# Scores of late attention pairs: two row-tiled matmuls per block replaced by one full-array matmul on a block-diagonal q^T

## The chip, the core and the metric

The kernel runs on one core of a Trainium2 chip. The metric is the device time of one launch in microseconds. The kernel before takes 220.62 us, the median of three runs (220.38 to 220.83). The profiled execution took 220.13 us, of which the profile's span covers 218.4 us.

The engines by their short names in the profile: PE is TensorE's matmuls, PEld its weight loads, DVE is VectorE, ACT is ScalarE, POOL is GpSimd, SP is SyncE, which here only issues transfers.

## The reference

Sinkhorn-sorted block attention, followed by a two-layer FFN with a squared ReLU. The batch B is 4, heads H 8, sequence S 768, head size D 64; the sequence falls into 8 blocks of 96.

```python
P = sort_net                                   # [4, 8, 8, 8]
for _ in range(5):                             # softmax-like steps on rows and columns
    P = exp(P - max(P)); P = P / sum(P, -1); P = P / sum(P, -2)
k_sorted = einsum('bhij,bhjcd->bhicd', P, k_blocks)
v_sorted = einsum('bhij,bhjcd->bhicd', P, v_blocks)
scores = matmul(q_blocks, k_sorted^T) / sqrt(D)          # inside each block of 96
attn = softmax(scores)
x = matmul(attn, v_sorted)                     # -> [3072, 512], heads side by side
h = maximum(x @ w_in, 0)                       # w_in  [512, 2048]
out = (h * h) @ w_out                          # w_out [2048, 512]
```

## The kernel before

Two heads are handled together as a "pair", so there are 16 units (b, hp). The kernel writes its operations into a plan, and a planner in Python orders them for each engine before anything is built. PE has two streams: the attention pieces and the FFN pieces ("chunks", 224 in all, each of four matmuls of 384 or 512 columns; the very last ones of eight of 256). Each attention piece has a *due* time, counted in FFN chunks:

```python
# Plan.run, the choice on PE (cut)
if sa is not None and (sf is None or sa < sf - 0.02
                       or (att[0].due <= chunks and sa <= sf + 0.1)):
    pick = (sa, att)          # attention piece at the head of its queue
elif sf is not None:
    pick = (sf, ffn)          # otherwise the next FFN piece
```

The due times are a table: for each batch and stage one number per pair or group. The stages are K, V, N (sorting of k and v), Z (transposes of k and q by DMA), S (scores), T (transpose of v), A (attention times v), X (transpose of the result), L (loads of the next batch).

Ten of the 16 units, pairs 2 and 3 of batch 1 and all of batches 2 and 3, are "late": their sorted k and their q are transposed by DMA, issued from SP:

```python
def s_turn(b, hp):                                       # cut
    nc.sync.dma_start_transpose(                         # kx: k^T of both heads, 128 rows
        out=kx_r[kx][:, 0:128 * NA].rearrange("p (a x) -> p a x", a=NA),
        in_=kn_r[m].rearrange("p a e d -> p (a e d)"))
    nc.vector.tensor_copy(out=qi_r[n]..., in_=qkv[b][0][:, 2*hp:2*hp+2, :]...)
    tiles["qT", b, hp] = att.tile([128, NA, 128], BF16, tag="qT", name="qT", bufs=6)
    nc.sync.dma_start_transpose(                         # q^T of both heads, 128 rows
        out=tiles["qT", b, hp], in_=qi_r[n].rearrange("p a e d -> p (a e d)"))
```

Rows 0 to 63 of kx and of q^T belong to the first head of the pair, rows 64 to 127 to the second. The scores of half a unit (4 blocks, 2 heads) are eight matmuls; each uses 64 rows of the array, so that the two heads can run side by side:

```python
# s_sc, for each half hf of the unit (cut); NQ = 4, C0 = 16, NB = 8, BLK = 96
for n in range(NQ):
    for h in range(2):
        nc.tensor.matmul(
            out=scp[:, h, BLK * n:BLK * (n + 1)],
            lhsT=kx_r[u.kx][64 * h:64 * (h + 1), NQ * hf + n::NB],     # late: every 8th column
            rhs=qT[64 * h:64 * (h + 1), :, C0 * (NQ * hf + n): C0 * (NQ * hf + n + 1)],
            start=True, stop=True)
```

In the early units the weights are `u.ksT[..., ... : ... + 128]`, contiguous, and `rhs` is contiguous too. ACT takes the exponential from PSUM into `et`, one activation of 384 columns per head. Then `s_av` multiplies by v, eight matmuls per half with `et` as the weights, 65 columns each, the 65th being the sum for the softmax:

```python
nc.tensor.matmul(out=oup[:, h, 66 * n:66 * n + D + 1],
                 lhsT=et_r[u.et[hf]][:, h, BLK * n:BLK * n + 128],
                 rhs=vb_r[w][:, NQ * hf + n, 2 * (u.hp % 2) + h, 0:D + 1], start=True, stop=True)
```

The result is transposed into xT, and the FFN reads xT: "up" is L958 (w_in as weights, 384 columns of xT), "down" is L988 (the squared activation as weights, 512 columns of w_out; L1016 at the end, 256 columns). The score matmuls are L651, attention times v is L838, the sorting of late k and v on 32x32 tiles of the array is L739. L413 is a filler matmul on ones that keeps PE at work while the first, latency-bound part runs.

Of the kernel before, what the change touches and what calls it, by code (L numbers as in the profile page):

```python
# [8 lines left out]
FP32 = mybir.dt.float32  # L9
# [9 lines left out]


DUES = {
    (0, "K"): (-79.0, -7.0, -34.5, 2.5),
    (0, "S"): (-13.5, 0.5, 6.0, 9.0),
    (0, "T"): (-30.5, -2.0, 4.5, 10.5),
    (0, "A"): (2.5, 14.5, 10.5, 12.5),
    (0, "X"): (4.5, 17.5, 19.0, 19.5),
    (0, "W"): (5.5,),
    (1, "V"): (18.5, 21.0),
    (1, "Q"): (21.0,),
    (1, "N"): (None, 27.0),  # L30
    (1, "Z"): (None, None, 42.0, 42.5),
    (1, "S"): (26.0, 38.5, 43.0, 49.5),
    (1, "A"): (42.0, 38.5, 44.0, 50.0),
    (1, "X"): (52.5, 47.5, 46.5, 51.5),
    (2, "L"): (66.0,),
    (2, "N"): (70.5, 75.5),
    (2, "V"): (67.0, 84.0),
    (2, "Z"): (76.0, 83.5, 78.0, 97.0),
    (2, "S"): (87.5, 93.5, 99.5, 100.0),
    (2, "A"): (91.0, 94.5, 100.0, 102.5),  # L40
    (2, "X"): (100.0, 109.5, 108.0, 104.0),
    (3, "L"): (109.5,),
    (3, "N"): (123.0, 127.0),
    (3, "V"): (123.0, 131.5),
    (3, "Z"): (127.0, 130.0, 127.5, 144.5),
    (3, "S"): (132.5, 145.5, 148.5, 158.0),
    (3, "A"): (138.0, 156.0, 161.5, 160.0),
    (3, "X"): (158.0, 156.0, 194.0, 265.0),
}


# [132 lines left out]
def kernel(  # L184
# [10 lines left out]
    nc = tc.nc  # L195
# [32 lines left out]

    plan = Plan()
    rvn, rvb = Ring(2), Ring(3)  # L230
    r1, r2, rf, rh1, rh2, rob = Ring(1), Ring(2), Ring(3), Ring(3), Ring(2), Ring(3)
    rqT, rao, rks, rvs, ret = Ring(6), Ring(3), Ring(3), Ring(3), Ring(4)
    rkx, rkn, rqi = Ring(3), Ring(4), Ring(4)
    AD = ("ACT", "DVE")

    def cost_f(n):
# [54 lines left out]

    kn_r = [const.tile([128, NA, 2, D], BF16, name=f"kn{n}") for n in range(4)]
    qi_r = [const.tile([128, NA, 2, D], BF16, name=f"qi{n}") for n in range(4)]
    kx_r = []
    for n in range(3):
        kx = const.tile([128, 128 * NB], BF16, name=f"kx{n}")
# [8 lines left out]
    w_in_bf = const.tile([128, KC, d_ff], BF16)  # L305
    w_out_bf = const.tile([128, NT, d_model], BF16)
    xT = const.tile([128, KC, n_tok], BF16)
    w_all = const.tile([128, NH // 2, NB, C0], BF16)
    w_t = const.tile([128, NH // 4, 4, NB], BF16)
    qkv = {}  # L310
    holds = {}
# [45 lines left out]
    def make_mask(e):  # L357

        src, w = ident, 64
        while w >= 4:  # L360
            dst = {C0: mask, 4: mask_t}.get(w) or const.tile([128, w], BF16, name=f"fold{w}")
            nc.gpsimd.tensor_tensor(out=dst, in0=src[:, 0:w], in1=src[:, w:2 * w], op=ALU.add)
            src, w = dst, w // 2
        nc.gpsimd.tensor_copy(out=mask_1.rearrange("p (z y) -> p z y", y=4),
                              in_=mask.rearrange("p (y z) -> p z y", z=4))

# [14 lines left out]
    rs = const.tile([NH, NB], FP32)  # L381
    cs = const.tile([NH, NB], FP32)
    pf = const.tile([NH, NB, NB], BF16)
    sel = const.tile([32, 32, C0], BF16)
    pt = const.tile([128, NB, NH], BF16)
    p_ij = const.tile([NH, 2, NH], BF16)

# [129 lines left out]
    def s_q(b, hp, p0, p1, due=0, after=None, eng=AD):  # L517

        n = p1 - p0
        t = {}  # L520

        def mm(e):
            qb = qkv[b][0]
            if b == 0:
                t["p"] = psf.tile([128, NA, n], BF16, tag="pf", name="qtp")
            else:
                t["p"] = ps1.tile([128, NA, n], BF16, tag="p1", name="qtp")
            for a in range(NA):
                for h in range(2):
                    nc.tensor.transpose(  # L530
                        out=t["p"][64 * h:64 * (h + 1), a, :],
                        in_=qb[p0:p1, 2 * hp + h, D * a:D * (a + 1)],
                        identity=ident[p0:p1, p0:p1])
            if p0 == 0:
                tiles["qT", b, hp] = att.tile(
                    [128, NA, 128], BF16, tag="qT", name="qT", bufs=6)

        def ev(e):
            qT, src = tiles["qT", b, hp].rearrange("p a x -> p (a x)"), t["p"]
            if b == 0:  # L540
                copy(e, qT.rearrange("p (i c a) -> p i c a", a=NA, c=C0)
                     [:, p0 // C0:p1 // C0, :, :], src.rearrange("p a (i c) -> p i c a", c=C0))
            else:
                copy(e, qT.rearrange("p (i a c) -> p i a c", a=NA, c=C0)
                     [:, p0 // C0:p1 // C0, :, :], src.rearrange("p a (i c) -> p i a c", c=C0))

        if b == 0:
            dep = landed[b, 0, 0, p0]
        else:
            dep = landed[b, 0, HP * (2 * hp // HP), 0]  # L550
        ring = rf if b == 0 else r1
        s1, old = ring.take()
        if p0 == 0:
            qTs[b, hp], oldq = rqT.take()
        else:
            oldq = []
        pe = plan.add("PE", 0.04 + 0.0023 * n, mm, [dep, id_op] + old, due, mode="col")
        readers[b].append(pe)
        op = one_of(eng, cost_b(NA * n), ev, [pe, after] + oldq)
        ring.use(s1, pe, op)  # L560
        rqT.use(qTs[b, hp], op)
        return op
# [72 lines left out]
    def s_sc(u, due=0):  # L635
# [3 lines left out]
        for hf in u.halves:  # L639
# [2 lines left out]
            slot, old = r2.take()  # L642

            def mm(e, hf=hf, st=st, slot=slot):
                qT = tiles["qT", u.b, u.hp]
                if not u.tiled:
                    qT = qT.rearrange("p a x -> p (a x)").rearrange("p (i q) -> p i q", q=BLK)
                st["p"] = scp = p2[slot]
                for n in range(NQ):
                    for h in range(2):  # L650
                        nc.tensor.matmul(  # L651
                            out=scp[:, h, BLK * n:BLK * (n + 1)],
                            lhsT=(u.ksT[64 * h:64 * (h + 1), HS * hf + BLK * n:HS * hf + BLK * n + 128]
                                  if not u.tiled else
                                  kx_r[u.kx][64 * h:64 * (h + 1), NQ * hf + n::NB]),
                            rhs=(qT[64 * h:64 * (h + 1), NQ * hf + n, :] if not u.tiled else
                                 qT[64 * h:64 * (h + 1), :, C0 * (NQ * hf + n):
                                    C0 * (NQ * hf + n + 1)]),
                            start=True, stop=True)

            s2 = slot
            u.et[hf], olde = ret.take()
            pe = plan.add("PE", 0.17 if not u.tiled else 0.26, mm, [u.k_op, u.q_op] + old, due,
                          mode="row")
            r2.use(s2, pe)
            rqT.use(qTs[u.b, u.hp], pe)
            if not u.tiled:
                rks.use(u.n, pe)
            else:
                rkx.use(u.kx, pe)  # L670
            u.exps[hf] = []
            if u.b == 0:
                def ex(e, st=st, et=et_r[u.et[hf]]):
# [6 lines left out]
                continue  # L680
            for h in range(2):
                def ex(e, h=h, st=st, et=et_r[u.et[hf]]):
                    nc.scalar.activation(  # L683
                        out=et[:, h, 0:HS].rearrange("p (n c a) -> p n c a", c=C0, a=NA),
                        in_=st["p"][0:96, h, 0:HS].rearrange("p (n a c) -> p n c a", c=C0, a=NA),
                        func=AF.Exp, scale=scale)
                op = plan.add("ACT", cost_f(HS)[0], ex, [pe] + olde)
                r2.use(s2, op)
                u.exps[hf].append(op)
# [91 lines left out]
    def loaded(b):  # L781
        return landed[b, 0, HP, 0]

    def s_turn(b, hp):
# [21 lines left out]
        qp = plan.add("DVE", 0.5, q_pair, [landed[b, 0, HP * (2 * hp // HP), 0]] + oldi)  # L806
        readers[b].append(qp)
        rqi.use(n, qp)
        qTs[b, hp], oldq = rqT.take()

        def q_turn(e):
            tiles["qT", b, hp] = att.tile([128, NA, 128], BF16, tag="qT", name="qT", bufs=6)
            nc.sync.dma_start_transpose(
                out=tiles["qT", b, hp], in_=qi_r[n].rearrange("p a e d -> p (a e d)"))

        sp = plan.add("SP", 1.35, q_turn, [qp, loaded(b)] + oldq)
        q_op = plan.add("WAY", 1.4, lambda e: None, [sp])
        rqi.use(n, q_op)
        rqT.use(qTs[b, hp], q_op)
        return kx, k_op, q_op  # L820

    def s_av(u, due=0):
        nao, olda = rao.take()
# [3 lines left out]
        for hf in u.halves:  # L827
# [4 lines left out]
            def mm(e, hf=hf, st=st, slot=slot):  # L832
# [3 lines left out]
                for n in range(NQ):  # L836
                    for h in range(2):
                        nc.tensor.matmul(  # L838
                            out=oup[:, h, 66 * n:66 * n + D + 1],
                            lhsT=et_r[u.et[hf]][:, h, BLK * n:BLK * n + 128],  # L840
                            rhs=(u.vs[:, NQ * hf + n, h, 0:D + 1] if u.b < 1 else
                                 vb_r[w][:, NQ * hf + n, 2 * (u.hp % 2) + h, 0:D + 1]),
                            start=True, stop=True)
# [83 lines left out]
    def put(key, t, n, dst, pe):  # L927
# [2 lines left out]
        so, old = rob.take()  # L930

        def cp(e):
            st["ob"] = ffn.tile([128, d_model], FP32, tag="ob", name="ob", bufs=3)
            copy(e, st["ob"][:, 0:n], t[key][:, 0:n])

        op = plan.add(AD, cost_f(n), cp, [pe] + old)
# [105 lines left out]
    builds = [build_w(h0, 4, pt, cp, i0, NQ, "POOL") for h0, i0 in ((4, 0), (0, NQ), (4, NQ))]  # L1042
    loads_after(builds[-1:])

    us = {}
    for name in FIRST.split():
        stage, n = name[0], int(name[1])
# [47 lines left out]

    def turn(b, hp, due):
        u = units[b, hp] = Unit(b, hp, (0, 1))
        u.kx, u.k_op, u.q_op = s_turn(b, hp)

    def load_late(b, n, due):  # L1100

# [62 lines left out]
```

## Time and profile before

| | before |
|---|---|
| device time, median | 220.62 us |
| span of the profile | 218.4 us |
| L958 PE, 506 matmuls | 88.8 us busy |
| L988 PE, 353 matmuls recorded | 82.4 us busy |
| L651 PE, late pairs, 160 matmuls | 7.1 us busy |
| L651 PE, early pairs, 96 matmuls | 3.6 us busy |
| L838 PE, 256 matmuls | 12.9 us busy |
| DVE, all | 102.3 us busy |
| ACT, all | 119.9 us busy |

A row of the groups names the line, the engine, the operation, out<-in by the names of the program, the shapes and the count; then the busy time and the mean of one in ns; then the idle time of the engine just before these instructions, and who ended it. PE's matmuls are pipelined: the next starts while the last one is still on its way through the array. So their durations overlap, and what a matmul costs in a stream is the time from its start to the next one's start, which the timeline shows. Some matmul records are missing from the trace: 353 of the 368 of L988 are there.

### The profile page before, as it was taken

Reading aid. Unit: us, or ns where it says so; the run is one execution under the profiler, and the core shown is the slowest. Engines: PE = TensorE matmul, PEld = TensorE weight load, DVE = VectorE, ACT = ScalarE, POOL = GpSimd, SP = SyncE. Lnnn points to the kernel's source line nnn. Section 1 sums busy time; section 2 is a strip of 40 time slices with the busy share of each in tenths; the row PEclk is TensorE's granted clock in tenths of the full one; section 3 lists DMA queues with packets and bytes.
Section 4 is the critical chain, followed back from the end, with each engine's and each line's share of the span. In section 5 each row is a group of like instructions: output and inputs, shape, how many; then the busy total and the mean of one; then the engine's idle time right before and its main releaser. Section 6 shows DMA issues by size and latency. Waiting matters only on the chain.

```text
span 218.4 us, 5137 instructions
## 1 busy us (share of the span) xinstructions
PE 211.8 (97%) x2067; PEld 120.8 (55%) x2082; DVE 102.3 (47%) x290; ACT 119.9 (55%) x249; POOL 28.4 (13%) x52
## 2 busy tenths in 40 slices
PE   8999999999999999999999999999999999999993
PEld 3676766446665555446655455446665565455552
DVE  6767578505693447504756057323656054015300
ACT  4666985427946178418782278229762375237321
POOL 7985221000000600000000510000000000000000
PEclk9999999999999999999999999999999999999999
DMA  5999999999494599189962699479864310120012
GB/s 68 191 201 207 207 207 214 202 221 302 79 181 107 85 231 214 17 230 174 231 172 55 147 195 214 99 182 173 191 171 112 99 46 0 48 96 3 0 64 80
DMA packets 46584, 31.22 MB, mean 143 GB/s; under 512 B 26017, under 2 KB 41633, under 8 KB 46561
## 3 DMA queue, kind: packets, MB, share of 16 engines
q0 software_dynamic: 12736, 13.63, 38.1%
q1 hardware_dynamic: 33824, 17.27, 34.6%
q8 instruction: 16, 0.26, 0.5%
q14 instruction: 8, 0.06, 0.1%
HBM read 29.70 MB, written 8.72 MB: 176 GB/s over the span
## 4 chain that ended last, share of the span: by engine, by line
PE 90%; DVE 4%; ACT 2%; issue 1%; DMA 1%; ACTq 0%; DVEq 0%
PE hp L958 38%; PE op L988 36%; PE p L651 4%; PE p L838 4%; PE p L739 2%; PE op L1016 2%; DVE p_sb L393 1%; PE p L616 1%; PE tp L580 1%; PE vbp L703 1%; DMA p_sb<-in_sort_net_dram 1%; PE xtp L889 1%; DVE cs L391 1%; ACT p_sb L425 1%; PE hp L916 1%
## 5 line engine op out<-in xcount | busy, mean ns | idle before, releaser
L958 PE MATMUL hp<-xT,w_in_bf 128*128 128x384 bf16 x506 | 88.8, 326 | 0.0
L988 PE MATMUL op<-w_out_bf,h 128*128 128x512 bf16 x353 | 82.4, 379 | 1.0 <-issue 0.3
L969 DVE TENSOR_TENSOR h<-h 128x384 bf16<-128x384 bf16 x128 | 44.3, 355 | 63.4 <-ACT h L966 62.7
L966 ACT ACTIVATE h<-hp 128x384 bf16<-128x384 f32 x128 | 61.6, 496 | 19.3 <-PE hp L958 14.6
L958 PEld LDWEIGHTS <-w_in_bf 128*128 128x128 bf16 x506 | 47.0, 98 | 31.0 <-issue 1.0
L988 PEld LDWEIGHTS <-h 128*128 128x128 bf16 x368 | 34.3, 98 | 38.2 <-issue 0.7
L247 ACT COPY ob<-op 128x512 f32<-128x512 f32 (+1 forms) x25 | 14.2, 568 | 55.9 <-PE op L988 53.3
L849 DVE TENSOR_TENSOR ao<-p,rec 96x512 bf16<-96x512 f32 x32 | 22.0, 687 | 1.1
L683 ACT ACTIVATE et<-p 96x384 bf16<-96x384 f32 x48 | 19.5, 493 | 3.5 <-PE p L651 1.9
L838 PEld LDWEIGHTS <-et 96*128 96x128 bf16 x256 | 11.7, 97 | 4.9 <-issue 0.4
L848 DVE RECIPROCAL rec<-p 96x8 f32<-96x8 f32 x32 | 6.4, 200 | 12.9 <-PE p L838 11.5
L1103 POOL COPY held<-xT 1x3 bf16<-1x3 bf16 (+1 forms) x2 | 0.4, 183 | 84.8 <-DMA xT<-ao 84.8
L413 PE MATMUL p<-ones 128*128 128x128 bf16 (+1 forms) x54 | 9.6, 317 | 1.1 <-DVE ones L268 1.1
L249 DVE CAST vn<-p 128x768 bf16<-128x768 f32 x6 | 5.7, 958 | 10.3 <-PE p L739 10.2
L838 PE MATMUL p<-vblk,et 96*128 96x65 bf16 x192 | 9.5, 193 | 0.0
L651 PEld LDWEIGHTS <-kx 64*128 64x128 bf16 x160 | 5.8, 155 | 3.6 <-issue 3.6
L249 DVE CAST kn<-p 128x768 bf16<-128x768 f32 x5 | 4.8, 958 | 6.1 <-PE p L739 6.1
L247 ACT CAST vn<-p 128x768 bf16<-128x768 f32 x6 | 4.8, 800 | 4.6 <-PE p L739 4.6
L413 PEld LDWEIGHTS <-ones 128*128 128x128 bf16 x54 | 4.4, 105 | 5.1 <-issue 2.5
L651 PE MATMUL p<-qT,kx 64*128 64x96 bf16 x160 | 7.1, 227 | 0.1
L318 POOL DMA_DIRECT2D kb<-in_k_dram x10 | 6.4, 643 | 4.4 <-DMA w_in_bf<-in_moe_w_in_dram 2.0
L318 POOL DMA_DIRECT2D qb<-in_q_dram x8 | 6.2, 770 | 4.9 <-DMA w_out_bf<-in_moe_w_out_dram 2.1
(80 smaller groups left out, 118.8 us busy)
## 6 DMA issues: line engine op xcount, KB each, us to landing
out_dram<-ob SPq DMA_DIRECT2D x23, 256.0 KB, 2.2
qb<-in_q_dram POOLq DMA_DIRECT2D x8, 384.0 KB, 11.6
v_way<-vn SPq DMA_DIRECT2D x6, 396.0 KB, 5.2
vblk<-v_way SPq DMA_DIRECT2D x6, 396.0 KB, 4.2
vb<-in_v_dram POOLq DMA_DIRECT2D x6, 384.0 KB, 12.5
kb<-in_k_dram POOLq DMA_DIRECT2D x6, 384.0 KB, 10.4
w_in_bf<-in_moe_w_in_dram POOLq DMA_DIRECT2D x4, 512.0 KB, 11.5
w_out_bf<-in_moe_w_out_dram POOLq DMA_DIRECT2D x4, 512.0 KB, 16.7
```

The source lines that it names most:

```text
L247: nc.scalar.copy(out=out, in_=in_)
L249: nc.vector.tensor_copy(out=out, in_=in_)
L318: nc.gpsimd.dma_start(out=dst, in_=src)
L413: nc.tensor.matmul(out=out, lhsT=ones, rhs=rhs, start=True, stop=True)
L651: nc.tensor.matmul(out=scp[:, h, BLK * n:BLK * (n + 1)], lhsT=(u.ksT[64 * h:64 * (h + 1), HS * hf + BLK * n:HS * hf + BLK * n + 128] if no ...
L683: nc.scalar.activation(out=et[:, h, 0:HS].rearrange("p (n c a) -> p n c a", c=C0, a=NA), in_=st["p"][0:96, h, 0:HS].rearrange("p (n a c) - ...
L838: nc.tensor.matmul(out=oup[:, h, 66 * n:66 * n + D + 1], lhsT=et_r[u.et[hf]][:, h, BLK * n:BLK * n + 128], rhs=(u.vs[:, NQ * hf + n, h, 0: ...
L849: nc.vector.tensor_tensor(out=u.ao[:, n0:n0 + NQ, :, :].rearrange("p n e d -> p e n d"), in0=ov[:, :, :, 0:D], in1=rec[:, :, :, None].to_b ...
L958: nc.tensor.matmul(out=t["hp", nt][:, 0:HS], lhsT=w_in_bf[:, kc, 128 * nt:128 * (nt + 1)], rhs=xT[:, kc, t0:t0 + HS], start=(kc == 0), sto ...
L966: nc.scalar.activation(out=t["h1", nt], in_=t["hp", nt][:, 0:HS], func=AF.Relu)
L969: nc.vector.tensor_tensor(out=t["h2"][:, nt, :], in0=t["h1", nt], in1=t["h1", nt], op=ALU.mult)
L988: nc.tensor.matmul(out=t["op", mt], lhsT=t["h2"][:, nt, 128 * mt:128 * (mt + 1)], rhs=w_out_bf[:, nt, :], start=(nt == 0), stop=(nt == NT ...
```

## The change

For the late pairs both heads go through the array in one matmul per block. q^T of the pair becomes a tile with two column parts: in part 0 the rows of the second head are zero, in part 1 those of the first. With k^T of both heads as the weights, all 128 rows, the 96 columns of part 0 give the first head's scores and the 96 of part 1 the second's. A unit then needs eight matmuls of 192 columns in full-array mode in place of sixteen of 96 columns in 64-row mode.

The zeros are written in two ways. The rows that stay zero for good, 0 to 63 of part 1, are set once on POOL for three tiles. The transpose by DMA fills part 0 with both heads; DVE then copies the second head's rows to part 1 and clears them in part 0. The exponentials and the weights of `s_av` follow the new order of the columns; there are as many of them, of the same sizes.

The aim is to be rid of the change of array mode around each late score block, which also lets the planner place half blocks freely. The due times were searched anew, so the order of much other work changes as well. To make room in SBUF, the ring of output buffers goes from 3 to 2, the ring of q^T tiles from 6 to 4 (only early units use it now), the selector of the first stage is put into a part of xT, and the sort weights' tile is cut to the heads that use it.

```diff
-    (1, "S"): (26.0, 38.5, 43.0, 49.5),
+    (1, "S"): (37.0, 42.5, 45.0, 49.5),
 ...                                             # the whole table of due times is new
-    (3, "N"): (123.0, 127.0),
-    (3, "V"): (123.0, 131.5),
-    (3, "Z"): (127.0, 130.0, 127.5, 144.5),
-    (3, "S"): (132.5, 145.5, 148.5, 158.0),
+    (3, "N"): (139.5, 137.0),
+    (3, "V"): (135.0, 141.0),
+    (3, "Z"): (142.5, 142.5, 144.5, 143.5),
+    (3, "S"): (143.5, 145.5, 158.0, 155.0),
 ...
-    r1, r2, rf, rh1, rh2, rob = Ring(1), Ring(2), Ring(3), Ring(3), Ring(2), Ring(3)
-    rqT, rao, rks, rvs, ret = Ring(6), Ring(3), Ring(3), Ring(3), Ring(4)
-    rkx, rkn, rqi = Ring(3), Ring(4), Ring(4)
+    r1, r2, rf, rh1, rh2, rob = Ring(1), Ring(2), Ring(3), Ring(3), Ring(2), Ring(2)
+    rqT, rao, rks, rvs, ret = Ring(4), Ring(3), Ring(3), Ring(3), Ring(4)
+    rkx, rkn, rqi, rqz = Ring(3), Ring(4), Ring(4), Ring(3)
 ...
+    qz_r = [const.tile([128, 2, NA, 128], BF16, name=f"qz{n}") for n in range(3)]
-    w_all = const.tile([128, NH // 2, NB, C0], BF16)
+    w_all = const.tile([128, H + HP, NB, C0], BF16)
-    sel = const.tile([32, 32, C0], BF16)
+    sel = xT[0:32, 0, 3 * S:3 * S + 32 * C0].rearrange("p (j c) -> p j c", c=C0)
 ...
+                if u.tiled:                                    # s_sc
+                    for n in range(NQ):
+                        i = NQ * hf + n
+                        nc.tensor.matmul(
+                            out=scp[:, n // 2, 2 * BLK * (n % 2):2 * BLK * (n % 2 + 1)],
+                            lhsT=kx_r[u.kx][:, i::NB],
+                            rhs=qz_r[u.qz][:, :, :, C0 * i:C0 * (i + 1)],
+                            start=True, stop=True)
+                    return
 ...
-            pe = plan.add("PE", 0.17 if not u.tiled else 0.26, mm, [u.k_op, u.q_op] + old, due,
-                          mode="row")
+            if u.tiled:
+                pe = plan.add("PE", 0.33, mm, [u.k_op, u.q_op] + old, due)
 ...
-                out=tiles["qT", b, hp], in_=qi_r[n].rearrange("p a e d -> p (a e d)"))
+                out=qz[:, 0, :, :], in_=qi_r[n].rearrange("p a e d -> p (a e d)"))
+
+        def q_split(e):
+            nc.vector.tensor_copy(out=qz[64:128, 1, :, :], in_=qz[64:128, 0, :, :])
+            nc.vector.memset(qz[64:128, 0, :, :], 0.0)
 ...
+        q_op = plan.add("DVE", 0.8, q_split, [q_op, zeros])
 ...
-                            lhsT=et_r[u.et[hf]][:, h, BLK * n:BLK * n + 128],
+                            lhsT=(et_r[u.et[hf]].rearrange("p h x -> p (h x)")
+                                  [:, BLK * (2 * n + h):BLK * (2 * n + h) + 128] if u.tiled else
+                                  et_r[u.et[hf]][:, h, BLK * n:BLK * n + 128]),
 ...
+    def make_zeros(e):
+        for qz in qz_r:
+            nc.gpsimd.memset(qz[0:64, 1, :, :], 0.0)
```

More of the change, by code (lines that the diff above doesn't have):

```diff
@@ L21 @@
 DUES = {
[L22 to L31, printed above, removed]
-    (1, "S"): (26.0, 38.5, 43.0, 49.5),
[L33 to L42, printed above, removed]
-    (3, "N"): (123.0, 127.0),
-    (3, "V"): (123.0, 131.5),
-    (3, "Z"): (127.0, 130.0, 127.5, 144.5),
-    (3, "S"): (132.5, 145.5, 148.5, 158.0),
-    (3, "A"): (138.0, 156.0, 161.5, 160.0),
-    (3, "X"): (158.0, 156.0, 194.0, 265.0),
+    (0, "K"): (-117.0, -41.5, -95.5, -25.5),
+    (0, "S"): (-43.0, -7.0, -66.5, -21.5),
+    (0, "T"): (-76.5, -17.5, -25.5, -2.5),
+    (0, "A"): (-10.0, -3.5, -25.5, 22.0),
+    (0, "X"): (19.0, 13.0, -2.0, 22.5),
+    (0, "W"): (-23.0,),
+    (1, "V"): (4.0, 18.0),
+    (1, "Q"): (32.0,),
+    (1, "N"): (None, 27.5),
+    (1, "Z"): (None, None, 35.0, 46.0),
+    (1, "S"): (37.0, 42.5, 45.0, 49.5),
+    (1, "A"): (40.0, 44.0, 46.5, 50.5),
+    (1, "X"): (43.5, 49.5, 46.5, 53.0),
+    (2, "L"): (64.0,),
+    (2, "N"): (71.0, 82.5),
+    (2, "V"): (65.5, 89.0),
+    (2, "Z"): (75.0, 90.5, 83.5, 93.5),
+    (2, "S"): (89.5, 95.0, 102.0, 95.5),
+    (2, "A"): (94.5, 95.0, 102.0, 96.0),
+    (2, "X"): (95.0, 104.0, 105.5, 96.0),
+    (3, "L"): (116.5,),
+    (3, "N"): (139.5, 137.0),
+    (3, "V"): (135.0, 141.0),
+    (3, "Z"): (142.5, 142.5, 144.5, 143.5),
+    (3, "S"): (143.5, 145.5, 158.0, 155.0),
+    (3, "A"): (143.5, 145.5, 162.0, 155.0),
+    (3, "X"): (157.0, 191.5, 195.5, 263.0),
 }
@@ L535, in mm @@
                 tiles["qT", b, hp] = att.tile(
-                    [128, NA, 128], BF16, tag="qT", name="qT", bufs=6)
+                    [128, NA, 128], BF16, tag="qT", name="qT", bufs=4)
         def ev(e):
@@ L644, in mm @@
             def mm(e, hf=hf, st=st, slot=slot):
-                qT = tiles["qT", u.b, u.hp]
-                if not u.tiled:
-                    qT = qT.rearrange("p a x -> p (a x)").rearrange("p (i q) -> p i q", q=BLK)
                 st["p"] = scp = p2[slot]
+                if u.tiled:
[7 more added lines that the diff above has]
+                    return
+                qT = (tiles["qT", u.b, u.hp].rearrange("p a x -> p (a x)")
+                      .rearrange("p (i q) -> p i q", q=BLK))
                 for n in range(NQ):
@@ L652, in mm @@
                             out=scp[:, h, BLK * n:BLK * (n + 1)],
[L653 to L658, printed above, removed]
+                            lhsT=u.ksT[64 * h:64 * (h + 1), HS * hf + BLK * n:HS * hf + BLK * n + 128],
+                            rhs=qT[64 * h:64 * (h + 1), NQ * hf + n, :],
                             start=True, stop=True)
@@ L662, in s_sc @@
             u.et[hf], olde = ret.take()
-            pe = plan.add("PE", 0.17 if not u.tiled else 0.26, mm, [u.k_op, u.q_op] + old, due,
-                          mode="row")
-            r2.use(s2, pe)
[L666 to L670, printed above, removed]
+            if u.tiled:
+                pe = plan.add("PE", 0.33, mm, [u.k_op, u.q_op] + old, due)
+                rkx.use(u.kx, pe)
+                rqz.use(u.qz, pe)
+            else:
+                pe = plan.add("PE", 0.17, mm, [u.k_op, u.q_op] + old, due, mode="row")
+                rqT.use(qTs[u.b, u.hp], pe)
+                rks.use(u.n, pe)
+            r2.use(s2, pe)
             u.exps[hf] = []
@@ L682, in ex @@
                 def ex(e, h=h, st=st, et=et_r[u.et[hf]]):
+                    if u.tiled:
+                        nc.scalar.activation(
+                            out=et.rearrange("p h x -> p (h x)")[:, HS * h:HS * (h + 1)]
+                            .rearrange("p (m c a) -> p m c a", c=C0, a=NA),
+                            in_=st["p"][0:96, h, 0:HS].rearrange("p (m a c) -> p m c a", c=C0, a=NA),
+                            func=AF.Exp, scale=scale)
+                        return
                     nc.scalar.activation(
@@ L808, in s_turn @@
         rqi.use(n, qp)
-        qTs[b, hp], oldq = rqT.take()
+        z, oldz = rqz.take()
+        qz = qz_r[z]
         def q_turn(e):
-            tiles["qT", b, hp] = att.tile([128, NA, 128], BF16, tag="qT", name="qT", bufs=6)
             nc.sync.dma_start_transpose(
-                out=tiles["qT", b, hp], in_=qi_r[n].rearrange("p a e d -> p (a e d)"))
-        sp = plan.add("SP", 1.35, q_turn, [qp, loaded(b)] + oldq)
+                out=qz[:, 0, :, :], in_=qi_r[n].rearrange("p a e d -> p (a e d)"))
+        def q_split(e):
+            nc.vector.tensor_copy(out=qz[64:128, 1, :, :], in_=qz[64:128, 0, :, :])
+            nc.vector.memset(qz[64:128, 0, :, :], 0.0)
+        sp = plan.add("SP", 1.35, q_turn, [qp, loaded(b)] + oldz)
         q_op = plan.add("WAY", 1.4, lambda e: None, [sp])
         rqi.use(n, q_op)
-        rqT.use(qTs[b, hp], q_op)
-        return kx, k_op, q_op
+        q_op = plan.add("DVE", 0.8, q_split, [q_op, zeros])
+        rqz.use(z, q_op)
+        return kx, z, k_op, q_op
     def s_av(u, due=0):
@@ L932, in cp @@
         def cp(e):
-            st["ob"] = ffn.tile([128, d_model], FP32, tag="ob", name="ob", bufs=3)
+            st["ob"] = ffn.tile([128, d_model], FP32, tag="ob", name="ob", bufs=2)
             copy(e, st["ob"][:, 0:n], t[key][:, 0:n])
@@ L1043 @@
     loads_after(builds[-1:])
+    def make_zeros(e):
+        for qz in qz_r:
+            nc.gpsimd.memset(qz[0:64, 1, :, :], 0.0)
+    zeros = plan.add("POOL", 1.5, make_zeros, builds[-1:])
     us = {}
@@ L1097, in turn @@
         u = units[b, hp] = Unit(b, hp, (0, 1))
-        u.kx, u.k_op, u.q_op = s_turn(b, hp)
+        u.kx, u.qz, u.k_op, u.q_op = s_turn(b, hp)
     def load_late(b, n, due):
```

## The prediction

> **What bounds the kernel now.** I began with the busy shares and the chain of work that ended last, on the page of the profile:
>
> ```profile
> span 218.4 us, 5137 instructions
> ...
> PE 211.8 (97%) x2067; PEld 120.8 (55%) x2082; DVE 102.3 (47%) x290; ACT 119.9 (55%) x249; POOL 28.4 (13%) x52
> ...
> PE 90%; DVE 4%; ACT 2%; issue 1%; DMA 1%; ACTq 0%; DVEq 0%
> ```
>
> TensorE carries the chain, and the other engines are busy about half of the span. A busy PE need not be a PE at its peak, so next I asked what it waits for. The answer of the waits, restricted to PE, is complete with these four lines:
>
> ```profile
> PE p L413 <- DVE ones L268: 1.1, 1, 1.1
> PE op L988 <- issue: 0.3, 2, 0.2
> PE hp L916 <- issue: 0.2, 1, 0.2
> PE pt L442 <- DVE p_ij L436: 0.2, 1, 0.2
> ```
>
> The columns are total us, times, longest us. Together 1.8 us, and 1.1 of it is the very start. From about 20 us on, when the FFN matmuls begin, PE hardly ever waits for another engine. So a change here pays only if it makes the PE stream itself shorter; a new schedule has almost no waits to take away, but it can add some.
>
> The changed stage is the scores of ten "late" pairs (two heads each). The groups, kept apart by shape:
>
> ```profile
> L651 PE MATMUL p<-qT,kx 64*128 64x96 bf16 x160 | 7.1, 227 | 0.1
> L651 PE MATMUL p<-qT,kvT 64*128 64x96 bf16 x96 | 3.6, 204 | 0.1
> L651 PEld LDWEIGHTS <-kx 64*128 64x128 bf16 x160 | 5.8, 155 | 3.6 <-issue 3.6
> L651 PEld LDWEIGHTS <-kvT 64*128 64x128 bf16 x96 | 2.4, 94 | 1.0 <-issue 0.3
> ```
>
> The kx rows are the late pairs, the kvT rows the same matmul for early pairs whose weights lie contiguous. Two things to see: a late weight load takes 155 ns, a contiguous one 94; and the weight loads idle 3.6 us ahead of the ten late blocks, put down to "issue", that is, to nothing that the profile shows another engine doing. Mean durations of pipelined matmuls are latencies, so I take costs from start to start, from the timeline of PE:
>
> ```profile
> 56.70 1.14 PE L958 MATMUL hp<-xT,w_in_bf 128*128 128x384 bf16 x6
> 57.77 0.51 PE L651 MATMUL p<-qT,kvT 64*128 64x96 bf16 x16
> 58.22 1.47 PE L958 MATMUL hp<-xT,w_in_bf 128*128 128x384 bf16 x8
> ...
> 99.77 1.14 PE L958 MATMUL hp<-xT,w_in_bf 128*128 128x384 bf16 x6
> 100.84 0.69 PE L651 MATMUL p<-qT,kx 64*128 64x96 bf16 x16
> 101.47 2.12 PE L958 MATMUL hp<-xT,w_in_bf 128*128 128x384 bf16 x12
> 103.43 0.41 PE L838 MATMUL p<-vblk,et 96*128 96x65 bf16 x8
> ```
>
> The first column is the start. Twelve matmuls of 384 columns take 103.43 - 101.47 = 1.96 us, 163 ns each. Six of them from 99.77 would end at 100.75; the score block starts at 100.84, so 0.09 us is lost on entering it. It holds the engine until 101.47, 0.63 us. A late unit costs PE 0.72 us. The contiguous block at 57.77 also loses 0.09 on entry and lasts 0.45: 0.54.
>
> **What the Trainium skill says.** "TensorEngine Tiling (Array Packing)", section Key Properties, says that changing the tiling mode, not just the tile, drains TensorE. The trace agrees: 0.09 us on entry to a 64-row block from a 128-row one, and the chain shows no wait there. "TensorE: Matmul & The Clock Gate", Back-to-back issue gap, gives columns/2.4 + 2.5 ns for a warm matmul; 163 ns for 384 columns agrees. Its step 1 of "Step-by-step" says the next weights may load in a background buffer while a matmul runs; the gapless 163 ns, with a load before each matmul, agree. "SBUF — State Buffer", in Door 1, speaks of 16-byte lines and a penalty for each access that crosses to a new one; kx is read with a step of 8 bf16, 16 bytes, and the 155 against 94 ns fit that.
>
> **The change part by part.**
>
> 1. *Scores of the late pairs.* Sixteen matmuls of 64 rows and 96 columns become eight of 128 rows and 192 columns. The half of the array that sees zeros in the block-diagonal q^T adds no time of its own. Cost of 192 columns: 384 columns take 163 ns and 512 take 216 (in the chain, eight of L988 take 1.73 us), so 0.416 ns a column and about 3 ns fixed: 80 + 3 = 83 ns. Eight give 0.66 us, and there is no drain on entry or exit, since the FFN is also in full-array mode. The strided weight load should hide. Evidence: two heads side by side, 96 columns, should need 0.416 x 96 + 3 = 43 ns, eight of them 0.34 us; the contiguous block took 0.54, so about 0.20 us is the switch in and out. The strided block took 0.72, so without the switch 0.52, or 65 ns a pair of matmuls. I read the 65 ns as the strided load, not the matmul, and 65 is under 83. So ten units go from 7.2 to 6.6 us: **-0.6 us**.
>
> 2. *Half blocks.* The changed program's order of PE instructions has 15 late score blocks instead of 10, some of four matmuls. In one mode this splitting is free.
>
> 3. *Other switches.* The new due times reorder the rest. Late scores aside, I counted the runs of consecutive non-full-array work between FFN matmuls. In batch 0 they stay as many; in batch 1 the early-pair scores split (16, 8, 8 instead of 16, 16) and the q transposes stand apart: one run more in all. At 0.20 us: **+0.2 us**. The eleven V and K sort blocks (L739) stay 16 matmuls each.
>
> 4. *Vector and Pool work.* Each late pair gets a copy and a memset of half a q tile. The existing copy of the same 768 columns (L802) takes 352 ns; for the memset I estimate up to 300 ns, from 165 ns for 256 columns of kx. Ten times 0.65 = 6.5 us, DVE 47% to 50%. The three memsets on POOL stand behind all batch-1 loads in its queue, at a time when it is idle. Off the path: 0.
>
> 5. *DVE in the q path.* Transpose, then split, then score: some 0.65 us later than today. I compared the PE order around the two stretches where it could show. In batch 3 the second K sort used to stand about 10 us ahead of the first score (139.5 and 149.8 in the chain); now between them lie four L988, four L958, one V sort and 24 L958, about 0.9 + 0.7 + 0.4 + 3.9 = 5.9 us. Needed: sort 0.3, evacuation about 1, transpose to landing 3.9 (median of the kx transposes), 5.2 in all. It fits with little left. In batch 2 the last pair's transposes queue behind the V write that waits for the second V sort; a similar sum leaves about half a microsecond. I allow **+0.1 us** on the mean for a stall here.
>
> 6. *Smaller rings.* The output buffer goes from 3 to 2. A tile of four L988 quarters takes 16 x 0.216 = 3.5 us, its output transfer lands in 2.2: hidden. The q^T ring of 4 serves early pairs only; the selector that now lives inside xT is read long before its columns are written. 0.
>
> Sum: -0.6 + 0.2 + 0.1 = -0.3 us; I take -0.5, because a searched order may also lose one or two of the 0.2 us stalls left in the stream. 220.6 - 0.5 = **220.1 us**.
>
> **The rivals.**
>
> A. *The matmul is slowed by its moving operand.* Today's late q^T is read in runs of 16 elements, the early one in one run of 96; so the 65 ns could be the moving side. Then 192 columns would take about 2 x 65 = 130 ns, eight 1.04 us, ten units 10.4: about +3 us, near 224. For it: the late matmul's mean is 227 ns against 204. Against: 23 ns is much less than the 61 ns by which the weight load grew, and a run of 16 elements is two whole lines of 16 bytes.
>
> B. *A new wait takes the place of the switch.* The transposes or the q split come too late for the tighter orders of point 5: PE would stand for 1 to 3 us, once or twice, 221 to 223. For it: transposes land in 2.5 to 6 us. Against: today's PE stream, laid out by the same planner with the same margins, shows no such wait.
>
> C. *The new due times are the larger gain.* The front, before 20 us, is latency-bound and could in principle give 1 us. Against: up to the second half-sort of batch 0 the PE order is unchanged, down to the number of fill matmuls. 219.
>
> **Range and chances.** The sure part is 0.6 us of 220.6. Low end: point 1 in full with some 1 us found in stalls, 219.0. High end: rival B with one stall of nearly 2 us, 221.9; rival A lies above it, at about one in fifteen. A gain of 2% would need 4.4 us, for which the stream has no room; a loss of 2% needs rival A stronger than drawn or several stalls.
>
> **What would show it.** The late score row should read x80 with a mean near 246 ns (193 for 65 columns plus 127 x 0.416), and start-to-start 0.66 us for eight; 1 us there means rival A. The idle of the weight loads at that line, 3.6 us, should go to almost nothing. The waits of PE should stay the four small lines; a line of the scores or of L838 waiting for a transpose or for the DVE copy means rival B. DVE should be near 108 us and its last wait unchanged. I am wrong if PE's span falls by over 1.5 us, or rises.

## The result and the profile after

The changed kernel takes 223.94 us (median of six runs, 222.65 to 224.87), the kernel before 220.71 in the same comparison: a ratio of 1.0146, 95% interval 1.0108 to 1.0184. It is about 3.2 us slower, and the predicted range ended at 221.9.

The page of the changed kernel, the same places as before:

```profile
span 223.0 us, 5002 instructions
...
PE 213.1 (96%) x2002; PEld 123.0 (55%) x2002; DVE 109.3 (49%) x308; ACT 121.4 (54%) x251; POOL 30.4 (14%) x55
...
PE 69%; DMA 22%; POOL 3%; ACT 2%; DVE 1%; issue 1%; SPq 0%; ACTq 0%
```

The busy shares hardly moved, which shows how little they tell. The chain did move: PE carried 90% of it before and carries 69% now, and 22% are transfers. A transfer on the chain counts with its whole length there, though PE works through most of it; the time lost is in the waits. What PE waits for says why (total us, times, longest us):

```profile
PE hp L979 <- ACT ob L247: 2.0, 1, 2.0
PE p L753 <- DMA vb<-in_v_dram: 1.3, 1, 1.3
PE p L415 <- DVE ones L268: 1.1, 1, 1.1
PE p L651 <- DVE ao L870: 0.9, 1, 0.9
PE p L857 <- DMA vblk<-v_way: 0.5, 1, 0.5
```

The third line was there before; the other four are new, 4.7 us together. This profile is of the slowest of the six runs, 224.87 us, so its loss is larger than that of the median. (L979 and L1009 are the FFN's up and down, L857 is attention times v, L753 the sorting of late k and v, L651 the late scores.) The scores themselves, first the group and then the timeline of PE around one unit:

```profile
L651 PE MATMUL p<-qz,kx 128*128 128x192 bf16 x80 | 9.2, 246 | 0.9 <-DVE ao L870 0.9
L651 PEld LDWEIGHTS <-kx 128*128 128x128 bf16 x80 | 8.5, 145 | 3.5 <-issue 1.8
```

```profile
105.87 1.47 PE L979 MATMUL hp<-xT,w_in_bf 128*128 128x384 bf16 x8
107.18 0.82 PE L651 MATMUL p<-qz,kx 128*128 128x192 bf16 x8
107.84 1.95 PE L979 MATMUL hp<-xT,w_in_bf 128*128 128x384 bf16 x11
```

Eight matmuls from 107.18 to 107.84 are 0.66 us, and 105.87 + 8 x 0.163 = 107.17: no loss on entry. A unit costs 0.66 us where it cost 0.72. So the change does to the scores what it was meant to do. One sign did not come: the idle time of the weight loads at this line is 3.5 us, as before, where almost nothing was forecast. PE's timeline shows no loss on entry all the same, so that idle time was no measure of the switch. The profiled loss of 223.0 - 218.4 = 4.6 us is these 4.7 us of waits, less 0.6 for the scores, plus small amounts.

**The largest wait** can be followed on the chain, in order of time (start, us, what):

```profile
42.21 0.56 ACT ob L247
42.76 0.02 issue
42.78 9.89 DMA out_dram<-ob
...
52.77 0.59 ACT ob L247
53.36 0.04 issue
53.41 2.76 PE hp L979 x16
```

The first output tile leaves at 42.78 and its transfer takes 9.89 us. With two buffers the third tile must wait for it; ACT stands 5.7 us, no PSUM buffer comes free, and PE stops. **The wait of the score** shows on DVE's timeline:

```profile
111.93 0.88 DVE L990 TENSOR_TENSOR h<-h 128x384 bf16<-128x384 bf16 x3
114.25 0.36 DVE L831 COPY qz<-qz 64x768 bf16<-64x768 bf16 x1 [1.44 <-DMA qz<-qi]
114.75 0.38 DVE L832 MEMSET qz<- 64x384 uint32 x1
...
115.67 0.69 DVE L870 TENSOR_TENSOR ao<-p,rec 96x512 bf16<-96x512 f32 x1
```

DVE stands 1.44 us at the q^T split, because the transpose has not landed. Behind it in DVE's queue is the normalisation that frees a PSUM slot, and the next score needs that slot:

```profile
116.41 0.49 PE L651 MATMUL p<-qz,kx 128*128 128x192 bf16 x4 [0.89 <-DVE ao L870]
```

It is the score of the very pair whose q^T was split. Its q was ready at 114.75 + 0.38 = 115.13, before PE was free at 116.41 - 0.89 = 115.52; the normalisation ended at 115.67 + 0.69 = 116.36. The Trainium skill says in "TensorE: Matmul & The Clock Gate", under the array's architectural detail, that VectorE's queue is strictly first in, first out; the trace agrees: DVE does nothing in those 1.44 us, although a matmul of attention times v from 113.55, whose normalisation stands behind the split, was done at 113.96.

### The profile page after: what moved, and what is told of

It is laid out like the page before. It is cut to its first block, busy times and chain, and to the rows that moved or that the text cites. A ratio compares the mean times of both kernels' runs of the same rounds, so it can differ in the third digit from the quotient of the medians.

```text
span 223.0 us, 5002 instructions
## 1 busy us (share of the span) xinstructions
PE 213.1 (96%) x2002; PEld 123.0 (55%) x2002; DVE 109.3 (49%) x308; ACT 121.4 (54%) x251; POOL 30.4 (14%) x55
## 4 chain that ended last, share of the span: by engine, by line
PE 69%; DMA 22%; POOL 3%; ACT 2%; DVE 1%; issue 1%; SPq 0%; ACTq 0%
PE op L1009 30%; PE hp L979 30%; DMA vb<-in_v_dram 9%; DMA out_dram<-ob 4%; DMA w_in_bf<-in_moe_w_in_dram 4%; PE p L651 2%; PE p L857 2%; DMA qz<-qi 2%; DMA vblk<-v_way 2%; PE op L1037 2%; PE p L753 1%; POOL kb L319 1%; POOL vb L319 1%; DMA p_sb<-in_sort_net_dram 1%; ACT ob L247 1%
## 5 line engine op out<-in xcount | busy, mean ns | idle before, releaser
L979 PE MATMUL hp<-xT,w_in_bf 128*128 128x384 bf16 x506 | 87.9, 326 | 2.0 <-ACT ob L247 2.0
L1009 PE MATMUL op<-w_out_bf,h 128*128 128x512 bf16 x368 | 85.2, 379 | 0.0
L979 PEld LDWEIGHTS <-w_in_bf 128*128 128x128 bf16 x506 | 47.9, 98 | 33.7 <-issue 3.0
L1009 PEld LDWEIGHTS <-h 128*128 128x128 bf16 x368 | 34.3, 98 | 36.6 <-issue 0.7
L247 ACT COPY ob<-op 128x512 f32<-128x512 f32 (+1 forms) x24 | 13.6, 567 | 53.9 <-PE op L1009 45.6
L691 ACT ACTIVATE et<-p 96x384 bf16<-96x384 f32 x40 | 16.8, 490 | 7.7 <-PE p L651 7.4
L857 PEld LDWEIGHTS <-et 96*128 96x128 bf16 x256 | 11.4, 97 | 4.8 <-issue 0.8
L651 PEld LDWEIGHTS <-kx 128*128 128x128 bf16 x80 | 8.5, 145 | 3.5 <-issue 1.8
L651 PE MATMUL p<-qz,kx 128*128 128x192 bf16 x80 | 9.2, 246 | 0.9 <-DVE ao L870 0.9
L857 PE MATMUL p<-vblk,et 96*128 96x65 bf16 x192 | 9.3, 193 | 0.5 <-DMA vblk<-v_way 0.5
L247 ACT CAST vn<-p 128x768 bf16<-128x768 f32 x6 | 4.8, 799 | 6.7 <-PE p L753 6.7
```

Of the source, the lines that this page charges most:

```text
L247: nc.scalar.copy(out=out, in_=in_)
L651: nc.tensor.matmul(out=scp[:, n // 2, 2 * BLK * (n % 2):2 * BLK * (n % 2 + 1)], lhsT=kx_r[u.kx][:, i::NB], rhs=qz_r[u.qz][:, :, :, C0 * i: ...
L691: nc.scalar.activation(out=et.rearrange("p h x -> p (h x)")[:, HS * h:HS * (h + 1)] .rearrange("p (m c a) -> p m c a", c=C0, a=NA), in_=st ...
L857: nc.tensor.matmul(out=oup[:, h, 66 * n:66 * n + D + 1], lhsT=(et_r[u.et[hf]].rearrange("p h x -> p (h x)") [:, BLK * (2 * n + h):BLK * (2 ...
L979: nc.tensor.matmul(out=t["hp", nt][:, 0:HS], lhsT=w_in_bf[:, kc, 128 * nt:128 * (nt + 1)], rhs=xT[:, kc, t0:t0 + HS], start=(kc == 0), sto ...
L1009: nc.tensor.matmul(out=t["op", mt], lhsT=t["h2"][:, nt, 128 * mt:128 * (mt + 1)], rhs=w_out_bf[:, nt, :], start=(nt == 0), stop=(nt == NT ...
```

## The experiments

The theory after this reading: the scores gain their 0.6 us, and four waits that the change let in cost more: output buffers, V load of batch 1, DVE's queue, attention values. The rival: the new order of work is too tight whatever the buffers are, or the new form of the scores costs time as such.

### 1. Three output buffers again

```diff
-            st["ob"] = ffn.tile([128, d_model], FP32, tag="ob", name="ob", bufs=2)
+            st["ob"] = ffn.tile([128, d_model], FP32, tag="ob", name="ob", bufs=3)
```

This is the main part of the edit; the rest only moves some tiles, as the expectation says.

> The changed kernel with three output buffers in SBUF instead of two; the planner still believes in two, so the order of instructions on every engine is that of the changed kernel. (To make room, the sort weights of batch 1 and some first-stage tiles lie inside tiles that are used only later.) Theory: the loss is four waits that the change let in, the largest of them the output buffer (PE waits 2.0 us near 51 us for ACT's copy, which waits for an output transfer). Then this wait is gone, the other three stay, and the time is 222.0 us (221.3 to 222.6), about 2 us under the changed kernel. Rival: the searched order asks for things too early in any case, and the same time is lost at the next wait (the transfers of batch 1): 223.3 us or more.

Measured 221.73 us (median of 20; against before 1.0042, interval 1.0023 to 1.0061), 2.2 us under the changed kernel. The waits of PE:

```profile
PE p L657 <- DVE ao L876: 1.0, 1, 1.0
PE hp L943 <- DMA w_in_bf<-in_moe_w_in_dram: 0.7, 1, 0.7
```

The output buffer's wait is gone, the score's wait on DVE stays. The V load's and the attention values' waits, which were to stay as well, are not in this profile. The second line is in the first, latency-bound part.

### 2. Two output buffers in the kernel before

```diff
-            st["ob"] = ffn.tile([128, d_model], FP32, tag="ob", name="ob", bufs=3)
+            st["ob"] = ffn.tile([128, d_model], FP32, tag="ob", name="ob", bufs=2)
```

> The kernel before with two output buffers in SBUF instead of three, the order of instructions unchanged. Theory: the third output tile near 49 us must wait for the first one's transfer, which is slow because the loads of batch 1 hold the DMA engines, so PE waits 1.5 to 3 us there and the time is 222.6 us (222.0 to 223.5). Rival: the old order leaves enough room and the smaller ring is harmless, as the prediction had it: 220.7 us.

Measured 223.98 us (1.0132, 1.0081 to 1.0184).

```profile
PE hp L958 <- ACT ob L247: 2.5, 1, 2.5
```

The ring alone, with the old order and the old scores, brings such a wait. This and the first experiment show it from both sides. But 223.98 us is more than the wait explains. The page gives TensorE's granted clock in 40 slices, in tenths of full speed:

```profile
PEclk9999999997999999999999999999999999999999
```

From 53.1 to 56.5 us (the 7 is the slice there), right behind the wait, the granted clock is 0.50: four matmuls of 384 columns take 53.16 to 54.53, 1.37 us, where four at 0.163 take 0.65. Half speed for 3.4 us is about 1.7 us lost (an estimate), and the first part is slower in this profile too. Two of the four runs have a mean clock of 0.992 and take 225.21 and 224.51 us; the two at 1.000 take 223.45 and 223.03, about 2.3 us above the 220.94 of before, which is what the wait alone would cost. The profiles of the changed kernel (wait of 2.0 us) and of experiment 9 (2.4 us) show no such fall, so what brings it is not shown.

### 3. The new due times alone

The kernel before with the new table.

> The kernel before (two 64-row matmuls per block, three output buffers) with the new table of due times and nothing else. It has 16 late score blocks instead of 10, so six more switches of the array mode at 0.2 us, 1.2 us, and one more early block, 0.2 us. Theory: beyond this it loses only the waits for the load of batch 1 (1.3 us) and for the attention values (0.5 us), not the output buffer's 2.0: 223.2 us (222.3 to 224.0), and PE waits for no DVE copy of q. Rival: the new order as such has no cost beyond the switches: 222.1 us or less.

Measured 223.66 us (1.0121, 1.0078 to 1.0164), inside the range of the theory, but with another wait than I had named:

```profile
PE p L838 <- DMA vblk<-v_way: 2.1, 2, 1.4
```

The V load's wait did not appear. With 64-row scores the new order splits the score blocks (16 instead of 10) and pays a switch for each. A half block there comes in 0.10 us late (107.71 + 8 x 0.163 = 109.01 against 109.11) and lasts 0.38: two cost 0.96 us where a whole one costs 0.72, so 0.24 us a split. It is an order for full-array scores; on its own it loses.

### 4. The new scores with the old due times

The changed kernel with the old table and three output buffers, planner and all.

> The changed scores, q tiles and DVE split with the old table of due times and three output buffers: the score change by itself. Theory: the score blocks cost 0.66 us a unit and the rest is as before, so 220.1 us (219.6 to 220.8), against 220.7 of the kernel before. Rival: the split on DVE, which waits there for a transfer and holds up all that stands behind it on that engine, costs by itself: 221.5 us or more.

Measured 224.46 us (1.0149, 1.0107 to 1.0190): a miss of 4 us. The planner had moved blocks, for its costs and rings are new:

```profile
PE p L863 <- ACT et L697: 1.4, 4, 0.4
```

It set attention times v directly behind its scores, and PE waits for the exponentials. There are more waits in the first part too. The run does not isolate the scores; it shows that due times, costs and rings belong together. Number 6 therefore holds the order fixed.

### 5. The split on POOL

From experiment 1, with the order of every engine but DVE and POOL kept:

```diff
-            nc.vector.tensor_copy(out=qz[64:128, 1, :, :], in_=qz[64:128, 0, :, :])
-            nc.vector.memset(qz[64:128, 0, :, :], 0.0)
+            nc.gpsimd.tensor_copy(out=qz[64:128, 1, :, :], in_=qz[64:128, 0, :, :])
+            nc.gpsimd.memset(qz[64:128, 0, :, :], 0.0)
```

> The changed kernel with three output buffers, and the split of q^T (copy and clear of half a tile) issued on POOL instead of DVE at the same place of the order; PE, ACT and SP keep their order. Theory: DVE takes its work in order, and the split at its head waits for a transfer, so everything behind it waits too; the one remaining PE wait of 1.0 us (a score that waits for DVE's normalisation, near 112 us) is of this kind and goes. Time 220.9 us (220.2 to 221.5) against 221.7 with the split on DVE. Rival: POOL is slower at it and the score then waits for POOL; 221.7 us or more.

Measured 220.46 us (median of 14), 0.9983 of before, interval 0.9962 to 1.0003: level with the kernel before within its interval. The waits of PE, complete:

```profile
PE p L421 <- DVE ones L268: 1.1, 1, 1.1
PE p L759 <- DMA vb<-in_v_dram: 0.4, 1, 0.4
PE hp L943 <- issue: 0.3, 1, 0.3
PE pt L450 <- DVE vblk L444: 0.2, 1, 0.2
PE op L1015 <- issue: 0.2, 1, 0.2
```

The score's wait is gone. POOL takes twice as long at it as DVE, and stands for it far longer:

```profile
L837 POOL COPY qz<-qz 64x768 bf16<-64x768 bf16 x10 | 8.3, 827 | 81.1 <-DMA qz<-qi 60.1 <-PE p L759 21.0
L838 POOL MEMSET qz<- 64x768 bf16 x10 | 7.3, 732 | 0.6
```

Those 60 us of waiting for the transposes cost PE nothing: PE waits for POOL nowhere in this profile. On DVE, 1.4 us of the same wait did cost something. From experiment 1 to this one the time falls by 1.3 us, with the intervals apart. One thing else differs: the transpose before this score lands after 4.4 to 4.5 us in the three profiles with the split on DVE (experiments 1 and 9, changed kernel), after 2.7 and 3.0 in the two on POOL (5 and 8). I did not settle why. With 4.5 us and about 1.7 us on POOL, the score would by estimate still have waited some 0.7 us, so part of what vanished may be the sooner landing.

### 6 and 7. The score change alone, in the old order

The planner is told the old costs, so the PE order is that of before but for one score block of batch 3, which stands one FFN piece, four matmuls, later (not 16 earlier, as the expectation of 6 says). It is also told that the split takes 0.01 us on POOL, so the order leaves no room for it. In 6 the split is on POOL, in 7 on DVE.

> The score change by itself: the PE order of the kernel before, except that one late score block stands 16 FFN matmuls earlier, three output buffers, full-array scores on the block-diagonal q^T, split on POOL. (The planner is told the old costs, so that it makes the old order.) Theory: each of ten units costs 0.66 us instead of 0.73 and nothing new is waited for, so 0.6 to 0.7 us less than the kernel before: 220.3 us (219.7 to 220.9) against 220.9. Rival: the form of the scores costs time wherever it stands; 221.5 us or more.

> The same kernel with the split on DVE, all else equal. Theory: DVE stands 1 to 2 us before a split whose transfer is under way, and its normalisations and squares come late, so PE waits in all 0.5 to 1.5 us: 221.2 us (220.7 to 222.0). Rival: in the old order the scores stand far enough behind the transposes, DVE's wait falls into its idle time, and the time is that of the split on POOL, 220.3 us.

Measured 222.13 us (1.0083, 1.0050 to 1.0116) and 224.95 us (1.0192, 1.0175 to 1.0209): both well over what I expected, and the number of the rival of 6 came in. First the wait of 6, then that of 7:

```profile
PE p L657 <- POOL qz L838: 1.7, 2, 0.9
```

```profile
PE p L657 <- DVE qz L838: 3.3, 2, 1.7
```

In the old order some scores stand right behind the landing of their q^T. The split comes between, and PE waits for the split itself. On DVE it waits longer: near 108.8 us two normalisations that stand before the split run until 107.86, which is not the wait for a transfer that the expectation named. So the new form of the scores needs a later place for them, which the new due times give: with them the same split on POOL (experiment 5) leaves no score waiting. What the new scores cost in an old order that leaves room for the split, these two runs do not show.

### 8. The split on POOL with two output buffers

> The changed kernel with the split on POOL and nothing else: still two output buffers. Theory: the waits are separate and add up; the output buffer's wait of 2.0 to 2.5 us near 51 us stays, the score that waits behind DVE goes. About 1.0 us less than the changed kernel's 223.9: 222.9 us (222.2 to 223.6). Rival: with PE late by the output buffer's wait anyway, DVE's delay hides behind it, or the reverse: 223.7 us or more.

Measured 223.05 us (1.0107, 1.0075 to 1.0138). The ring's wait is there (`PE hp L979 <- ACT ob L247`, 1.9 us), the score's is not. The medians differ from the changed kernel's by 0.9 us, but the intervals overlap, so the size is not clear of noise; the ring, from experiment 8 to 5, is 2.6 us here. That the two add up roughly fits, and is not shown more exactly.

### 9. The changed kernel once more

> The changed kernel once more, for a second profile: which of the four waits come back. Theory: the output buffer's wait (2.0 to 2.6 us) and the score's wait behind DVE (0.9 to 1.2 us) are of the program and come back; the waits for the V load of batch 1 (1.3 us) and for the attention values (0.5 us) hang on when transfers land and may be absent. Time between 222.6 and 224.9 us.

One run, 224.1 us.

```profile
PE hp L979 <- ACT ob L247: 2.4, 1, 2.4
PE p L651 <- DVE ao L870: 1.0, 1, 1.0
PE p L753 <- DMA vb<-in_v_dram: 0.2, 1, 0.2
```

Ring and DVE queue come back, the V load's wait shrinks from 1.3 to 0.2, the attention values' is gone. The first two came in both profiles and are of the program; the others change from run to run.

### 10 and 11. Looking for a better version

Both start from experiment 5. In 10 the planner is told of the ring of three and of 1.6 us on POOL:

> Three output buffers and the split on POOL as in the best variant so far (220.5 us), but with the planner told of both: a ring of three, and 1.6 us on POOL for the split instead of 0.8 on DVE. It then places several scores and some sort blocks one or two FFN pieces later. Theory: the PE stream has the same work and the waits left are under 1 us in all, so it ends within 0.4 us of 220.5, and varies less from run to run. Rival: the later scores push attention times v and the transposes of the result against the next batch's loads, and time is lost: 221.2 us or more.

In 11 the V sorts of batch 1 are due later:

```diff
-    (1, "V"): (4.0, 18.0),
+    (1, "V"): (20.0, 21.0),
```

> The variant with three output buffers and the split on POOL, with the due times of batch 1's V sorts at 20 and 21 instead of 4 and 18, so that the first V sort on PE stands one FFN piece later (0.9 us), behind the landing of its load; some later blocks move too. Theory: the wait for that load (0.4 us in the profile of the best variant) goes: 220.1 us (219.7 to 220.6). Rival: the later V sort delays its way through memory and attention times v of batch 1 waits instead: 220.9 us or more.

Measured 221.25 us (1.0035, 1.0019 to 1.0051) and 227.55 us (1.0307, 1.0284 to 1.0329). In number both are at or over the rivals. In 10 PE waits 0.6 us for a transposed result, the direction of its rival, and the runs vary as before (220.48 to 223.08), not less. In 11 the V load's wait is gone as expected, and attention times v of batch 1 does not wait, as the rival had it; but the planner shifted later blocks too, and near 175 us the FFN waits for the transposed results:

```profile
PE hp L985 <- DMA xT<-ao: 4.3, 2, 3.6
```

Behind the 3.6 us the granted clock is 0.50 from 177.6 to 184.4 us, by estimate another 2.9 us; with the waits that makes most of the 7.1 us over experiment 5. So a later place for attention work, which experiments 6 and 7 asked for, can be overdone: the results must be back before the FFN of that half batch. No version that clearly beats the kernel before came out; experiment 5 is level with it.

## Why the prediction was wrong, point by point

- *What bounds the kernel.* Right, and so was the warning drawn from it, that a new schedule could add waits but hardly remove any. I then sized the waits to be added far too small, and "the waits of PE should stay the four small lines" failed.
- *Point 1, the scores.* Right in size: 83 ns a matmul predicted, 82.5 from start to start; 0.66 us a unit; mean 246 ns as forecast. The strided load takes 145 ns against 98 for a contiguous one and hides. Rival A, the slow moving operand, is refuted.
- *Points 2 and 3.* Four-matmul blocks did come without an entry cost: one takes 0.33 us, half of 0.66. With 64-row scores a split costs 0.24 us (experiment 3). The extra switches of the other blocks (0.2 us) were not measured apart.
- *Point 4, DVE's work.* The copy took 350 ns as predicted; the memset 378 instead of up to 300; DVE 109.3 us against 108. "Off the path: 0" was wrong. I counted the 0.7 us of work and not the 1.4 us for which the split, waiting for its transfer, holds up DVE's queue. In three profiles PE waits 0.9 to 1.0 us for it; experiment 5 wins 1.3 us, perhaps in part by a sooner landing.
- *Point 5, q path.* The place was right: the last pair of batch 2. So was the margin: the split was done 0.4 us before PE was free, where about half a microsecond was forecast. The error was to follow only the score's own q. What stands behind the split in DVE's queue was left out, and there is the normalisation that frees the score's PSUM slot, 0.8 us later than PE was free. The term of 0.1 us came out at 0.9 to 1.0. In the old order (6 and 7) the split itself is what the score waits for.
- *Point 6, smaller rings.* **The step that failed most.** The tile "takes 16 x 0.216 = 3.5 us, its output transfer lands in 2.2: hidden": this used the median landing over the whole kernel. The first output tiles leave while the loads of batch 1 are under way, and there a transfer took 9.9 us. Of three buffers or two, that is the difference between none and 2.0 to 2.5 us of PE waiting (experiments 1 and 2), and 2.2 us of the median. The trace of before had it already, for the output transfers between 36 and 60 us:

```profile
L937 SPq DMA_DIRECT2D out_dram<-ob x3: 338/377/719, 41.6 to 49.1; - x3
DMA to landing us min/median/max: 5.0/7.9/9.8
48.53 0.58 ACT L247 COPY ob<-op 128x512 f32<-128x512 f32 x1 [2.87 <-PE op L988]
```

The first is issued at 41.6 and lands 9.8 us later, at 51.4. The third tile's copy starts at 48.53 and with two buffers would have had to wait 2.9 us for it.
- *The rivals.* B was the right kind, a new wait in place of the switch. Its own part, transposes and split, came to 0.9 to 1.0 us, the low end of its "1 to 3 us, once or twice"; the ring, the larger wait, was not in it. C did not happen in the front.
- *Still open.* The V load of batch 1 lands about when PE asks for it; its wait was 1.3, 0.2 or 0.4 us in three profiles and absent in that of experiment 1. I didn't settle what moves the landing. Why the granted clock halves behind some waits and not behind others is open too. Nor is it shown what experiment 6 would take without its 1.7 us of split waits. From 0.06 us a unit a gain of a few tenths of a us is likely, but experiment 5 is only 0.25 us under the kernel before, which is not clear of noise.

## What to carry to other kernels

Where PE never waits, what a change frees is small and what it crowds out can be large: check every buffer that was given up for it, with the landing time of *that* stretch, not the median. An instruction that waits for a transfer belongs on an engine whose queue holds nothing urgent behind it; its own duration is the lesser cost. A table of due times is tuned to the costs, rings and engines it was searched with, so change them together and measure each apart with the order held fixed.

## What was not expected of the hardware

The same 256 KB output transfer lands in 2.1 us at the median and in 9.9 us while the loads of batch 1 are under way. After a wait of PE of 2.5 us (experiment 2) and one of 3.6 us (experiment 11) the granted clock was 0.50 for 3.4 and 6.8 us; after waits of 2.0 and 2.4 us (changed kernel, experiment 9) it stayed full. In the profile of experiment 6 it was 0.50 from 15.0 to 21.5 us, behind a wait of 0.7 us (for the V load), so the length of the wait alone does not decide it. The strided load of 128x128 weights (step of 16 bytes) has the longer duration in full-array mode too, 145 against 98 ns, and costs nothing behind a matmul of 192 columns.
